# Cross-covariance attention and channel mix on one core: squares in quads, an earlier v, and units dealt out anew

## The chip, the cores and the metric

The kernel runs on one core of a Trainium2 chip. The metric is the device time of one execution in microseconds; the number given for a kernel is the median of several executions.

## The reference

The inputs are q, k and v of shape (4, 6208, 256) in float32, and the weights of a channel mix. For each of the four batches, with norms taken along the sequence of 6,208 rows:

```
qn, kn = q / (norm(q, axis=1) + 1e-6), k / (norm(k, axis=1) + 1e-6)
a = softmax(kn.T @ qn / tau)             # 256 x 256
x = v @ a
x_prev = x shifted by one row, zeros first
xk = mu_k * x + (1 - mu_k) * x_prev      # the same with mu_r for xr
out = sigmoid(xr @ w_r) * (relu(xk @ w_k) ** 2 @ w_v)
```

Here w_k is 256 x 1024, w_v 1024 x 256 and w_r 256 x 256. The output is float32. On the chip the matmuls run on bf16.

## The kernel before, in words

A batch has 12 blocks of 512 rows and 64 rows left over. The 48 blocks, and one block of the 4 x 64 leftover rows, go through the channel mix. Everything is issued in an order written out by hand.

**The head.** Batch 0's q and k are loaded through SP's queue in float32, cast by VectorE and ScalarE, and multiplied into the 256 x 256 covariance; its norms are made by TensorE from squares. A softmax follows, and the first x.

**The loop.** Pass i of the main loop has eight steps, j = 0 to 7. In it block i+1 is multiplied up: in each step `up` makes one 128 x 512 slice of the hidden layer (two matmuls into a `kT_ps` bank, of which there are three), and ScalarE's relu (L423) writes it to a tile `kr`. A step later, in every second step, `square` lets VectorE square the two slices of a `kr` tile into `kk` (L429). Block i is multiplied down: `down` makes, in two steps, w_r's product (L444) and w_v's over the eight slices of `kk` (L448) for 128 rows, in one of two `vr_ps` banks; `finish` takes a tanh on ScalarE (L457), a product on VectorE (L458), and the store through SP's queue. The squares of a block's last slices are made in step 0 of the pass that multiplies it down. For block i+2, `x_half` makes x (two halves in steps 0 and 2, L348 and L350), and VectorE makes the shifted difference `delta` (L394) and the two mixes `xk` and `xr` (L404).

**v.** `v_load` loads a block through POOL's queue with a cast to bf16, five passes before that block's pass, into one of five buffers. `v_transpose` turns it by a DMA transpose on SP's queue, four passes before, into one of four `vT` buffers. Blocks 0, 1 and 2 are turned by TensorE instead (`v_transpose_pe`, L327), through a `kT_ps` bank and a copy (L331).

**The next batches.** While the loop runs, batches 1 to 3 get their covariances. A batch is 49 units: 48 of 128 rows and one of the 64 leftover rows. `group_load` loads q and k of four units through POOL's queue with a cast, into a tile whose rows alternate q and k. `unit_matmul` makes two matmuls of 256 columns for a unit (L167), accumulating in one bank, `s_ps`. `unit_square` squares two units at once on ScalarE (L150) into float32, and `next_add` adds this to the running sum `acc` on VectorE (L154), in steps 1, 6 and 7 at most while no softmax is due. In which steps a pass issues a unit stands in `slots`; five units are multiplied ahead of pass 0. After a batch's last unit, `softmax_pieces` gives a list of pieces of which each step issues one: `evac` copies the covariance out, `fold` folds the sum of squares, `norms` to `spread` make and spread the inverse norms, then scaling, exponential, and `weigh`, which writes the matrix `a_sb` (L273) that `x_half` of the next batch reads.

The order of pieces and the slots, as they stand:

```
return [evac, None, fold, None, norms, roots, roots2, None, invert, None, spread, scale,
        None if bounded else top, exp, None, weigh]
...
elif i < 8:
    slots = (1, 2, 3, 4, 5, 7)
else:
    slots = (3, 5, 7) if (i - 8) % NB == 0 else (1, 3, 4, 5, 7) if (i - 8) % NB < 3 else (1, 3, 5, 7)
```

Of the kernel before, what the change touches and what calls it, by code (L numbers as in the profile page):

```python
# [18 lines left out]
def kernel(  # L19
# [76 lines left out]
    def order(b):  # L96
        g = list(range(len(sizes(b))))
        return [1, 2, 0] + g[3:] if b == 0 else g

# [10 lines left out]
    def group_load(b, g):  # L110
        rows, n = rows_of(b, g)
        qk = pq.tile([P, S, 2, C], BF16, name="qk", tag="qk", bufs=5)
        groups[b, g] = (qk,)
        if b == 0:
            qk2 = pq.tile([P, S, 2, C], BF16, name="qk2", tag="qk2", bufs=4)
            groups[b, g] += (qk2,)
            t_f = []
            for i, t in enumerate((q, k)):
                f = pq.tile([P, S, C], F32, name=f"f{i}", tag=f"f{i}", bufs=6)
                nc.sync.dma_start(f[:rows, :n], qk_src(t, b, g))  # L120
                t_f.append(f)
            groups[b, g] += tuple(t_f)
        else:
            for i, t in enumerate((q, k)):
                nc.gpsimd.dma_start(qk[:rows, :n, i, :], qk_src(t, b, g))  # L125

    def group_cast(b, g):
        rows, n = rows_of(b, g)
        qk, qk2, *t_f = groups[b, g]
        for i in range(2):  # L130
            nc.vector.tensor_copy(qk[:rows, :n, i, :], t_f[i][:rows, :n])  # L131
        for i in range(2):
            nc.scalar.activation(qk2[:rows, :n, i, :], t_f[i][:rows, :n], AF.Square)  # L133

    def unit_square(b, g, s):

        rows, n = rows_of(b, g)
        if s % 2:
            return
        qk = groups[b, g][0]  # L140
        if n == 1:
            t = pq.tile([P, 1, 2 * C], BF16, name="sq", tag="sq1", bufs=2)
            sums[b, "left"] = t
        elif (g, s) == (1, 0):
            t = pn.tile([P, 2, 2 * C], F32, name="acc", tag="acc", bufs=2)
            sums[b] = t
        else:
            t = pq.tile([P, 2, 2 * C], F32, name="sq2", tag=f"f{s // 2}", bufs=6)
            adds.append((now[0] + 2, b, t))
        nc.scalar.activation(t[:rows], qk[:rows, s:s + min(n, 2)].rearrange("p s i c -> p s (i c)"), AF.Square)  # L150

# [4 lines left out]
    def unit_matmul(b, g, s):  # L156
# [9 lines left out]
        for ih in range(2):  # L166
            nc.tensor.matmul(s_ps[:, ih, :], qk[:rows, s, 1, ih * P:(ih + 1) * P],  # L167
                             qk[:rows, s, 0, :], start=t0 and ih == 0, stop=te,
                             skip_group_check=True)
# [28 lines left out]
    def softmax_pieces(b):  # L198
# [20 lines left out]
        def fold():  # L219
            t = pq.tile([P, 2 * C], BF16, name="sq", tag="sq", bufs=1)  # L220
            nc.vector.tensor_tensor(t, sums[b][:, 0], sums[b][:, 1], op=OP.add)
            sums[b] = t

        def norms():
            bank[b] = ps.tile([P, 2 * C], F32, name="bank", tag="xT_ps", bufs=2)
            for t, rows in ((sums.pop((b, "left"))[:, 0], L), (sums.pop(b), P)):
# [64 lines left out]
        if b == 0:  # L291
            return [copies, gather, roots, evac, invert, spread, halves]

        return [evac, None, fold, None, norms, roots, roots2, None, invert, None, spread, scale,
                None if bounded else top, exp, None, weigh]

# [23 lines left out]

    def v_transpose_pe(i, evac):
# [7 lines left out]
        def go():  # L329
            vT = p2.tile([P, S, 2, P], BF16, name="vT", tag="vT", bufs=4)  # L330
            evac(vT, vT_ps)  # L331
# [80 lines left out]
    def up(i, fh):  # L412
# [5 lines left out]
        for dh in range(2):  # L418
            nc.tensor.matmul(kT_ps[:, :m], w_k_sb[:, dh, fh * P:(fh + 1) * P], xk[:, dh, :m],  # L419
                             start=dh == 0, stop=dh == 1)  # L420
        if fh % 2 == 0:
            st[i, "kr", fh // 2] = p2.tile([P, 2, M], BF16, name="kr", tag="kr", bufs=3)
        nc.scalar.activation(st[i, "kr", fh // 2][:, fh % 2, :m], kT_ps[:, :m], AF.Relu, scale=0.5 ** 0.5)  # L423

    def square(i, fh):
        m = size(i)
        if fh % 2:
            kr = st.pop((i, "kr", fh // 2))[:, :, :m]
            nc.vector.tensor_tensor(st[i, "kk"][:, fh - 1:fh + 1, :m], kr, kr, op=OP.mult)  # L429

# [90 lines left out]

    units = [(b, g, s) for b in range(1, B) for g in range(NB + 1) for s in range(sizes(b)[g])]
    loads = [(b, g) for b in range(1, B) for g in range(NB + 1)]
    AHEAD = 3
# [7 lines left out]
    def loads_upto():  # L532
# [3 lines left out]
        b, g, _ = units[min(n, len(units) - 1)]  # L536
        at = (b - 1) * (NB + 1) + g
        while loads and pos["ld"] <= at + AHEAD:
# [3 lines left out]
    chain = []  # L542
    FOLD = 14
    holds = [0]

    def unit(ahead=2):
# [9 lines left out]
        if u[1:] == (NB, S - 1):  # L556
            chain.extend(softmax_pieces(u[0]))
            holds[0] = u[0]

# [27 lines left out]

    early = units[:S + 1]
    pos["mm"] = pos["sq"] = S + 1

# [109 lines left out]
```

## Time and profile before

| | |
|---|---|
| median of 4 runs | 514.84 us (514.65 to 515.66) |
| the profiled execution's own time | 514.48 us |
| its span | 512.7 us |
| TensorE busy | 489.2 us, 95% of the span |
| VectorE busy | 457.2 us, 89% |
| ScalarE busy | 431.3 us, 84% |
| GpSimd busy | 104.5 us, 20% |
| granted TensorE clock | 1.00 |
| DMA packets, data moved | 143,734, 83.72 MB |

The profiled execution is one run; the span reaches from its first to its last instruction. Busy time is the time in which at least one instruction of an engine is under way. Matmuls are pipelined and overlap, and so do the ends of instructions on VectorE and ScalarE with the start of the next, so that the mean duration of an instruction is longer than its spacing to the next one. The first matmul of the main loop (pass -1) starts 44.8 us into the span.

### The profile page before, as it was taken

The numbers are of one execution on the slowest core, as the hardware profiler recorded it, in microseconds if no ns is written. First come the engines' busy times: TensorE is split into PE (matmuls) and PEld (weight loads), VectorE is DVE, ScalarE is ACT, GpSimd is POOL, SyncE is SP. The second block draws the span as 40 slices with busy tenths as digits, with TensorE's granted clock in tenths as the row PEclk, the third lists the DMA queues.
The fourth block names the chain that finished last, engine by engine and source line by source line (L and its number), as shares of the span: only waits on it lengthen the run. The fifth ranks groups of instructions, "written<-read, shape, count | busy, mean of one in ns | idle before, by whom it ended". The sixth has DMA issues, their size and how long they took to land.

```text
span 512.7 us, 9442 instructions
## 1 busy us (share of the span) xinstructions
PE 489.2 (95%) x3447; PEld 332.4 (65%) x3509; DVE 457.2 (89%) x788; ACT 431.3 (84%) x858; POOL 104.5 (20%) x143
## 2 busy tenths in 40 slices
PE   3989999999999999999999999999999999999996
PEld 1454566666666676677676667667666666666675
DVE  4557899999999999999999999999989787888884
ACT  5886999989888888888988889889877888878784
POOL 0046252322252222212152321210030110000000
PEclk9999999999999999999999999999999999999999
DMA  8999999999979999989899999964279756424123
GB/s 315 420 310 193 190 194 195 222 158 182 189 106 203 188 152 197 141 145 173 134 145 183 201 155 197 167 120 110 63 117 172 134 117 128 103 77 109 42 83 102
DMA packets 143734, 83.72 MB, mean 163 GB/s; under 512 B 51716, under 2 KB 140104, under 8 KB 143688
## 3 DMA queue, kind: packets, MB, share of 16 engines
q0 software_dynamic: 65808, 33.01, 51.9%
q1 hardware_dynamic: 77712, 49.98, 39.6%
q8 instruction: 27, 0.44, 0.4%
q10 hardware_dynamic: 168, 0.13, 0.1%
q14 instruction: 19, 0.16, 0.1%
HBM read 78.71 MB, written 25.43 MB: 203 GB/s over the span
## 4 chain that ended last, share of the span: by engine, by line
PE 68%; DVE 20%; DMA 5%; ACT 3%; issue 2%; SPq 1%; DVEq 0%; ACTq 0%
PE vr_ps L448 26%; PE kT_ps L419 23%; PE vr_ps L444 8%; PE xT_ps L348 6%; DVE acc L154 6%; DMA f<-in_k_dram 5%; DVE kk L429 5%; PE s_ps L167 4%; DVE xk L404 3%; DVE res L458 2%; DVE xr L404 2%; DVE delta L394 1%; ACT kr L423 1%; SPq L120 1%; ACT sq L150 1%
## 5 line engine op out<-in xcount | busy, mean ns | idle before, releaser
L423 ACT ACTIVATE kr<-kT_ps 128x512 bf16<-128x512 f32 (+1 forms) x392 | 233.9, 601 | 39.4 <-PE kT_ps L419 35.6
L448 PE MATMUL vr_ps<-w_v_sb,kk 128*128 128x256 bf16 x1536 | 231.8, 273 | 0.9 <-DVE kk L429 0.3
L419 PE MATMUL kT_ps<-xk,w_k_sb 128*128 128x512 bf16 (+1 forms) x725 | 218.4, 377 | 0.3 <-DVE xk L404 0.2
L448 PEld LDWEIGHTS <-kk 128*128 128x128 bf16 x1536 | 149.5, 98 | 60.3 <-DVE kk L429 3.2
L429 DVE TENSOR_TENSOR kk<-kr 128x1024 bf16<-128x1024 bf16 (+1 forms) x196 | 132.8, 677 | 3.7 <-ACT kr L423 2.8
L458 DVE SCALAR_TENSOR_TENSOR res<-res,vr_ps 128x256 f32<-128x256 f32 x192 | 79.4, 414 | 27.3 <-ACT res L457 26.9
L419 PEld LDWEIGHTS <-w_k_sb 128*128 128x128 bf16 x784 | 76.1, 98 | 28.7 <-issue 0.5
L154 DVE TENSOR_TENSOR acc<-acc,sq 128x1024 f32<-128x1024 f32 x69 | 83.9, 1216 | 0.0
L167 PE MATMUL s_ps<-qk 128*128 128x256 bf16 (+1 forms) x392 | 72.4, 285 | 4.9 <-DVE qk L131 4.8
L457 ACT ACTIVATE res<-vr_ps 128x256 f32<-128x256 f32 x192 | 75.5, 393 | 1.3 <-PE vr_ps L448 1.3
L444 PE MATMUL vr_ps<-w_r_sb,xr 128*128 128x256 bf16 x384 | 73.2, 272 | 3.3 <-DVE res L458 0.5
L350 ACT CAST xT<-xT_ps 128x512 bf16<-128x512 f32 x94 | 55.9, 594 | 23.2 <-PE xT_ps L348 23.0
L150 ACT ACTIVATE sq<-qk 128x1024 f32<-128x1024 bf16 (+1 forms) x72 | 75.2, 1046 | 0.0
L404 DVE SCALAR_TENSOR_TENSOR xr<-delta,mu_t,xT 128x512 bf16<-128x512 bf16 x96 | 71.3, 743 | 0.0
L404 DVE SCALAR_TENSOR_TENSOR xk<-delta,mu_t,xT 128x512 bf16<-128x512 bf16 x96 | 71.2, 743 | 0.0
L444 PEld LDWEIGHTS <-xr 128*128 128x128 bf16 x384 | 37.5, 98 | 45.6 <-issue 1.6
L125 POOL DMA_DIRECT2D qk<-in_q_dram x39 | 28.7, 735 | 181.4 <-ACT kr L423 140.6
L348 PE MATMUL xT_ps<-vT,a_sb 128*128 128x512 bf16 x188 | 56.1, 379 | 3.4 <-DVE a_sb L273 2.2
L311 POOL DMA_DIRECT2D v_bf<-in_v_dram x48 | 37.2, 776 | 63.9 <-DMA vT<-v_bf 61.6
L167 PEld LDWEIGHTS <-qk 128*128 128x128 bf16 (+1 forms) x392 | 38.3, 101 | 16.8 <-DVE qk L131 7.7
L394 DVE TENSOR_TENSOR delta<-xT 128x1024 bf16<-128x1024 bf16 x48 | 32.8, 684 | 0.1
L133 ACT ACTIVATE qk<-f 128x1024 bf16<-128x1024 f32 (+2 forms) x28 | 25.9, 948 | 7.1 <-DMA f<-in_q_dram 5.4
(82 smaller groups left out, 164.0 us busy)
## 6 DMA issues: line engine op xcount, KB each, us to landing
out_dram<-res SPq DMA_DIRECT2D x47, 512.0 KB, 4.2
v_bf<-in_v_dram POOLq DMA_DIRECT2D x48, 256.0 KB, 7.6
qk<-in_q_dram POOLq DMA_DIRECT2D x36, 256.0 KB, 6.0
qk<-in_k_dram POOLq DMA_DIRECT2D x36, 256.0 KB, 7.0
f<-in_q_dram SPq DMA_DIRECT2D x11, 512.0 KB, 8.4
f<-in_k_dram SPq DMA_DIRECT2D x11, 512.0 KB, 9.3
vT<-v_bf SPq DMA_TRANSPOSE x45, 7.3
f<-in_q_dram SPq DMA_DIRECT2D x2, 256.0 KB, 8.4
```

What stands on the lines that cost most here:

```text
L150: nc.scalar.activation(t[:rows], qk[:rows, s:s + min(n, 2)].rearrange("p s i c -> p s (i c)"), AF.Square)
L154: nc.vector.tensor_tensor(sums[b], sums[b], t, op=OP.add)
L167: nc.tensor.matmul(s_ps[:, ih, :], qk[:rows, s, 1, ih * P:(ih + 1) * P], qk[:rows, s, 0, :], start=t0 and ih == 0, stop=te, skip_group_che ...
L348: nc.tensor.matmul(xT_ps, a_sb[:, b, ih, dh * P:(dh + 1) * P], vT[:, :, ih, :], start=ih == 0, stop=ih == 1)
L404: nc.vector.scalar_tensor_tensor(o[:, dh], st[i, "d"][:, dh], mu[:, dh:dh + 1], st[i, "x"][:, dh, :M], op0=OP.mult, op1=OP.add)
L419: nc.tensor.matmul(kT_ps[:, :m], w_k_sb[:, dh, fh * P:(fh + 1) * P], xk[:, dh, :m], start=dh == 0, stop=dh == 1)
L423: nc.scalar.activation(st[i, "kr", fh // 2][:, fh % 2, :m], kT_ps[:, :m], AF.Relu, scale=0.5 ** 0.5)
L429: nc.vector.tensor_tensor(st[i, "kk"][:, fh - 1:fh + 1, :m], kr, kr, op=OP.mult)
L444: nc.tensor.matmul(vr_ps[:, D:], xr[:, dh, s * P:(s + 1) * P], w_r_sb[:, dh, :], start=dh == 0, stop=dh == 1)
L448: nc.tensor.matmul(vr_ps[:, :D], kk[:, fh, s * P:(s + 1) * P], w_v_sb[:, fh, :], start=fh == 0, stop=fh == 7)
L457: nc.scalar.activation(res[:, s], vr_ps[:, D:], AF.Tanh, scale=0.5)
L458: nc.vector.scalar_tensor_tensor(res[:, s], res[:, s], 1.0, vr_ps[:, :D], op0=OP.add, op1=OP.mult)
```

## The change

The change has five parts.

- The squares of relu: `kr` holds four slices instead of two, in two buffers instead of three, and VectorE squares four at once. For blocks 1 to 33 slice 0 is squared by ScalarE, right after its relu, and VectorE's first square takes slices 1 to 3. The block of leftover rows keeps pairs.
- q and k lie apart in their tile: all q rows of a partition, then all k rows. The tiles of squares follow this layout.
- v is loaded six passes ahead into six buffers and transposed five ahead into five. Block 3 is turned by TensorE, in pass 0. The loads ahead of the loop are issued in another order.
- The leftover rows come third in each batch, not first, and the units are dealt to other steps: four ahead of the loop, then 3, 6, 6, 7, 7, 7, 7 and so on.
- The softmax's list has 17 pieces in another spacing, with `fold` right after `evac`, and no unit is issued in the four steps after a batch's last.

```diff
-        return [1, 2, 0] + g[3:] if b == 0 else g
+        return [1, 2, 0] + g[3:]
...
-        qk = pq.tile([P, S, 2, C], BF16, name="qk", tag="qk", bufs=5)
+        qk = pq.tile([P, 2, S, C], BF16, name="qk", tag="qk", bufs=5)
...
-                nc.gpsimd.dma_start(qk[:rows, :n, i, :], qk_src(t, b, g))
+                nc.gpsimd.dma_start(qk[:rows, i, :n, :], qk_src(t, b, g))
...
-        return [evac, None, fold, None, norms, roots, roots2, None, invert, None, spread, scale,
-                None if bounded else top, exp, None, weigh]
+        return [evac, fold, None, None, norms, roots, roots2, None, None, invert, None, None, spread,
+                scale, *([] if bounded else [top]), exp, None, weigh]
...
-        v_bf = p2.tile([P, S, C], BF16, name="v_bf", tag="v_bf", bufs=5)
+        v_bf = p2.tile([P, S, C], BF16, name="v_bf", tag="v_bf", bufs=6)
...
-        vT = p2.tile([P, S, 2, P], BF16, name="vT", tag="vT", bufs=4)
+        vT = p2.tile([P, S, 2, P], BF16, name="vT", tag="vT", bufs=5)
...
-        if fh % 2 == 0:
-            st[i, "kr", fh // 2] = p2.tile([P, 2, M], BF16, name="kr", tag="kr", bufs=3)
-        nc.scalar.activation(st[i, "kr", fh // 2][:, fh % 2, :m], kT_ps[:, :m], AF.Relu, scale=0.5 ** 0.5)
+        if fh % 4 == 0:
+            st[i, "kr", fh // 4] = p2.tile([P, 4, M], BF16, name="kr", tag="kr", bufs=2)
+        kr = st[i, "kr", fh // 4][:, fh % 4, :m]
+        nc.scalar.activation(kr, kT_ps[:, :m], AF.Relu, scale=0.5 ** 0.5)
+        if fh == 0 and by_act(i):
+            nc.scalar.activation(st[i, "kk"][:, 0, :m], kr, AF.Square)
+
+    def by_act(i):
+        return 1 <= i < 3 * NB - 2
 
     def square(i, fh):
         m = size(i)
-        if fh % 2:
-            kr = st.pop((i, "kr", fh // 2))[:, :, :m]
-            nc.vector.tensor_tensor(st[i, "kk"][:, fh - 1:fh + 1, :m], kr, kr, op=OP.mult)
+        n = 4 if i < NBLK - 1 else 2
+        if fh % n == n - 1:
+            lo = 1 if fh == 3 and by_act(i) else fh % 4 + 1 - n
+            kr = st[i, "kr", fh // 4][:, lo:fh % 4 + 1, :m]
+            nc.vector.tensor_tensor(st[i, "kk"][:, fh // 4 * 4 + lo:fh + 1, :m], kr, kr, op=OP.mult)
...
-    FOLD = 14
-    holds = [0]
+    FOLD = 16 if bounded else 17
+    holds = [0, 0]
...
-            holds[0] = u[0]
+            holds[:] = u[0], now[0] + 4
...
-    next_load()
     v_load(1)
     next_load()
...
+    v_load(2)
     nc.gpsimd.dma_start(w_v_sb, moe_w_v.rearrange("(fo fi) d -> fi fo d", fi=P))
-    v_load(2)
-    next_load()
+    v_load(3)
...
-    early = units[:S + 1]
-    pos["mm"] = pos["sq"] = S + 1
+    early = units[:S]
+    pos["mm"] = pos["sq"] = S
...
-            if j == 0 and 3 <= i + 5 < NBLK - 1:
-                v_load(i + 5)
+            if j == 0 and i + 6 < NBLK - 1:
+                if i < 0:
+                    next_load()
+                v_load(i + 6)
...
-            if j == 5 and 3 <= i + 4 < NBLK - 1:
-                v_transpose(i + 4)
+            if i == 0 and j == 6:
+                v_transpose_pe(3, nc.vector.tensor_copy)()
+            if j == 5 and 4 <= i + 5 < NBLK - 1:
+                v_transpose(i + 5)
...
-            if (i, j) in ((0, 1), (0, 5), (1, 3)):
-                unit_square(*early[{(0, 1): 0, (0, 5): 1, (1, 3): 3}[i, j]])
+            if (i, j) in ((0, 1), (0, 3)):
+                unit_square(*early[{(0, 1): 0, (0, 3): 2}[i, j]])
...
-                slots = (3, 5, 7)
-            elif i == 1:
-                slots = (1, 2, 4, 5, 7)
-            elif i < 8:
-                slots = (1, 2, 3, 4, 5, 7)
+                slots = (5, 6, 7)
+            elif i < 7:
+                slots = (1, 2, 3, 4, 5, 7) if i < 3 else (1, 2, 3, 4, 5, 6, 7)
+            elif i == 7:
+                slots = (1, 2, 7)
+            elif (i - 7) % NB == 0:
+                slots = (5, 7)
             else:
-                slots = (3, 5, 7) if (i - 8) % NB == 0 else (1, 3, 4, 5, 7) if (i - 8) % NB < 3 else (1, 3, 5, 7)
-            if j in slots and pos["mm"] < len(units):
+                slots = (1, 3, 4, 5, 7) if (i - 7) % NB in (1, 3, 6, 9) else (1, 3, 5, 7)
+            if j in slots and pos["mm"] < len(units) and now[0] >= holds[1]:
                 unit()
```

More of the change, by code (lines that the diff above doesn't have):

```diff
@@ L130, in group_cast @@
         for i in range(2):
-            nc.vector.tensor_copy(qk[:rows, :n, i, :], t_f[i][:rows, :n])
+            nc.vector.tensor_copy(qk[:rows, i, :n, :], t_f[i][:rows, :n])
         for i in range(2):
@@ L141, in unit_square @@
         if n == 1:
-            t = pq.tile([P, 1, 2 * C], BF16, name="sq", tag="sq1", bufs=2)
+            t = pq.tile([P, 2, 1, C], BF16, name="sq", tag="sq1", bufs=2)
             sums[b, "left"] = t
         elif (g, s) == (1, 0):
-            t = pn.tile([P, 2, 2 * C], F32, name="acc", tag="acc", bufs=2)
+            t = pn.tile([P, 2, 2, C], F32, name="acc", tag="acc", bufs=2)
             sums[b] = t
         else:
-            t = pq.tile([P, 2, 2 * C], F32, name="sq2", tag=f"f{s // 2}", bufs=6)
+            t = pq.tile([P, 2, 2, C], F32, name="sq2", tag=f"f{s // 2}", bufs=6)
             adds.append((now[0] + 2, b, t))
-        nc.scalar.activation(t[:rows], qk[:rows, s:s + min(n, 2)].rearrange("p s i c -> p s (i c)"), AF.Square)
+        nc.scalar.activation(t[:rows], qk[:rows, :, s:s + min(n, 2)], AF.Square)
     def next_add():
@@ L166, in unit_matmul @@
         for ih in range(2):
-            nc.tensor.matmul(s_ps[:, ih, :], qk[:rows, s, 1, ih * P:(ih + 1) * P],
-                             qk[:rows, s, 0, :], start=t0 and ih == 0, stop=te,
+            nc.tensor.matmul(s_ps[:, ih, :], qk[:rows, 1, s, ih * P:(ih + 1) * P],
+                             qk[:rows, 0, s, :], start=t0 and ih == 0, stop=te,
                              skip_group_check=True)
@@ L219, in fold @@
         def fold():
-            t = pq.tile([P, 2 * C], BF16, name="sq", tag="sq", bufs=1)
-            nc.vector.tensor_tensor(t, sums[b][:, 0], sums[b][:, 1], op=OP.add)
+            t = pq.tile([P, 2, C], BF16, name="sq", tag="sq", bufs=1)
+            nc.vector.tensor_tensor(t, sums[b][:, :, 0], sums[b][:, :, 1], op=OP.add)
             sums[b] = t
@@ L225, in norms @@
             bank[b] = ps.tile([P, 2 * C], F32, name="bank", tag="xT_ps", bufs=2)
-            for t, rows in ((sums.pop((b, "left"))[:, 0], L), (sums.pop(b), P)):
+            for t, rows in ((sums.pop((b, "left")).rearrange("p i s c -> p (i s c)"), L),
+                            (sums.pop(b).rearrange("p i c -> p (i c)"), P)):
                 for i in range(4):
@@ L329, in go @@
         def go():
-            vT = p2.tile([P, S, 2, P], BF16, name="vT", tag="vT", bufs=4)
+            vT = p2.tile([P, S, 2, P], BF16, name="vT", tag="vT", bufs=5)
             evac(vT, vT_ps)
@@ L520 @@
             v_load(0)
-    units = [(b, g, s) for b in range(1, B) for g in range(NB + 1) for s in range(sizes(b)[g])]
-    loads = [(b, g) for b in range(1, B) for g in range(NB + 1)]
+    units = [(b, g, s) for b in range(1, B) for g in order(b) for s in range(sizes(b)[g])]
+    loads = [(b, g) for b in range(1, B) for g in order(b)]
     AHEAD = 3
@@ L536, in loads_upto @@
         b, g, _ = units[min(n, len(units) - 1)]
-        at = (b - 1) * (NB + 1) + g
+        at = (b - 1) * (NB + 1) + order(b).index(g)
         while loads and pos["ld"] <= at + AHEAD:
```

## The prediction

> **What bounds the kernel now.** I read the page first (TensorE busy 489.2 of 512.7 us, VectorE 457.2), then cut the span at the starts of the loop's passes and asked for the busy time of each engine in these stretches, then the chain and the waits inside them. Pass i multiplies block i+1 up and block i down. Four passes, columns as in the page's engines (busy us and instruction count), then clock, DMA share, GB/s:
>
> ```profile
> 81.60:92.00 10.40, 10.27 (x74) 6.95 (x73) 10.40 (x17) 9.32 (x19) 1.47 (x2) 1.00 1.38 195
> ...
> 154.20:165.20 11.00, 10.04 (x72) 6.85 (x72) 10.96 (x21) 9.64 (x19) 2.23 (x3) 1.00 1.37 211
> ...
> 184.50:194.00 9.50, 9.45 (x69) 6.61 (x68) 9.29 (x16) 8.39 (x18) 2.82 (x4) 1.00 1.00 152
> ...
> 404.80:413.50 8.70, 8.65 (x61) 5.89 (x61) 7.27 (x14) 7.08 (x16) 0.78 (x1) 1.00 0.64 122
> ```
>
> TensorE looks full in all four, so its busy share tells nothing; the length of a pass does. The last has no covariance unit, the third 4, the first 6. One pass is 20 matmuls of 512 columns and 40 of 256. In the chain a pair of the former takes 0.43 us and five of the latter 0.55, so a pass needs 20 x 0.216 + 40 x 0.109 = 8.68 us, and each unit (two of 256) 0.218 more. Without units the pass is 8.7 us long and with four 9.56 (floor 9.55): TensorE at its floor. With six the floor is 9.99, yet passes 2 to 6 take 10.39. Why, the chain says:
>
> ```profile
> 82.14 1.14 DVE acc L154
> ...
> 86.01 0.33 DVE res L458
> 86.34 1.14 DVE acc L154
> 87.48 0.60 DVE kk L429
> 88.08 0.66 DVE xr L404
> 88.74 0.33 DVE res L458
> 89.07 0.60 DVE delta L394
> ...
> 91.27 0.67 DVE xk L404
> ```
>
> Pure VectorE. These times are spacings to the next instruction (the profile's means run about 0.08 longer, since the ends overlap). A pass is one delta 0.60, four squares 2.41, two xk and two xr 2.65, four res 1.32 = 6.98 us, and 1.135 for each running add; with three adds 10.39, the length of the pass. So VectorE bounds passes 1 to 8 (61 to 144 us) and pass 10 (11.0 us: three adds and the last softmax piece, 6.98 + 3.41 + 0.53). At the end of each softmax TensorE also waits for it:
>
> ```profile
> PEld L348 <- DVE a_sb L273: 3.5, 6, 1.2
> PE xT_ps L348 <- DVE a_sb L273: 2.2, 3, 0.9
> PE xT_ps L348 <- DMA vT<-v_bf: 0.4, 1, 0.4
> ```
>
> The third is block 3's transpose, landing late, once. Summing length less floor, passes 0 to 34 hold about 9 us to win; the passes after are at the floor and the 44.8 us head is a stream of loads.
>
> [...] the trace has the shape:
>
> ```profile
> L150 ACT ACTIVATE sq<-qk 64x512 bf16<-64x512 bf16 x3 | 1.9, 618 | 0.0
> ```
>
> [...]
>
> **The change, part by part.**
> *Squares in quads.* Blocks 1 to 33: four DVE squares (2.41 us) become one of 1,536 elements and one of 2,048. No such size is in the trace; at 0.52 ns per element and a fixed 0.07 (from 0.60 for 1,024) I take 0.87 + 1.135 = 2.00, so 0.40 less per pass; the other blocks save 0.14. Bounds: nothing saved (if a long one runs slower), or 0.45. Added on ScalarE: one Square of 512, 0.52, plus about 0.11 because it reads what the instruction ahead has just written (in the head an xk that follows its delta so started 0.72 after it, not 0.60): 0.63, bounds 0.5 to 0.9. Behind it on ScalarE stand the xT copy, the next relu and the tanh; VectorE and TensorE wait for these. ScalarE holds 8 relus 3.95, two xT 0.96, four tanh 1.10, a copy 0.08 and 0.47 per unit: 8.0 us with four units before, 8.6 of 9.56 after; with seven 10.04 of 10.21. It fits, narrowly there. The later squares of a block come in one piece at the next pass's first step: 1.13 instead of 0.60, but the pair before is gone from the queue ahead of it. At 186.60 that pair's square started 1.3 us ahead of its reader; the quad would begin about 0.6 earlier and end with some 0.5 to spare. Cost nothing while VectorE has slack; without it, up to 0.5 a pass.
>
> *Units regrouped.* 4 instead of 5 before the loop, then 3, 6, 6, 7, 7, 7, 7, 2: batch 1 ends in pass 7 step 2, not step 7; batch 2 at the end of pass 18, not 19; batch 3 in pass 30, not 31. No unit is added or lost. The running adds are still three a pass at most, so VectorE needs 6.58 + 3.41 = 9.99 in passes 1 to 6, against floors of 9.99 (6 units) and 10.21 (7): both engines level, TensorE ahead. The softmax chain grows from 16 to 17 pieces but starts 5, 8 and 10 steps earlier, so its last piece comes some 5 or more steps ahead of its use, not one: the a_sb waits go. What is late next there is VectorE in pass 7 (three adds and the fold, about 11.0 us of work in a pass with floor 9.4), which I let leak 0.5.
> The four-step hold on new units spares a wait on the single s_ps bank; it costs no work.
>
> *Block 3 on TensorE.* Eight transposes of 128 columns, 8 x 0.056 = 0.45, and a VectorE copy 0.60 in pass 0. VectorE is busy 7.7 of 9.9 there, which hides the copy; if not, TensorE waits 0.8 as it did for block 2's. Off: a DMA transpose, its SP issue and the 0.4 wait. Pass 0 is ScalarE's: squares 4 x 0.95 + 0.52, relus, copies, and now the new Square: 10.5 us of work against 9.9 long before. I put it at 10.2.
>
> *v one block further ahead, six and five buffers.* The same POOL and SP issues, earlier: POOL's 0.78 per v load and two of 0.73 per group move past each other in the head. w_v comes behind one v block (256 KB, some 1.3 us by the gaps between landings): it landed at 48.3, would at about 49.6, and is first read at 53.7. Group 1 moves ahead of the leftover rows and needs nothing later. Cost nothing; if that cover went, 1 us once. TensorE waits nowhere else on v, so nothing is won either.
> *q and k apart.* Each row of a partition becomes one 2 KB piece instead of four of 512 B: 36,864 packets of 143,734 fall to about 9,200. No engine waits on these loads after the head: nothing, either way.
>
> **The sum**, by pass. Pass -1: 6.0 (6.2). Pass 0: 10.2 (9.9). 1 and 2: 10.1 each. 3 to 6: 10.3 each. 7: 9.9; 8: 10.3; 9: 9.7; 10: 9.85; 11: 9.6. Together 126.9, before 130.1 (44.8 to 174.9): 3.2 off. Passes 12 to 23: 12 x 8.68 + 50 x 0.218 + 0.7 for the softmax's and leftover matmuls + 0.3 of stalls = 116.1, before 117.2: 1.1 off. Passes 24 to 34: 11 x 8.68 + 29 x 0.218 + 1.0 = 102.8, before 104.0: 1.2 off. The last pass waits for one quad more, +0.2 (estimate); ScalarE's fuller queue, +0.5 over 33 passes (estimate). Net 4.8. The profiled execution took 514.48 around a span of 512.7, 0.36 under the median of the runs; so its like would be 509.7 and the median 514.84 - 4.8 = **510.1 us**.
>
> **The rivals.**
> *A, as summed* (0.68): 510.1, own range 508 to 512.
> *B, ScalarE hands part of it back* (0.14): with 8.6 to 10.0 us in each pass it lags after the 0.95 us squares, and TensorE meets it at the next free kT_ps bank, 0.08 a pass: 33 x 0.08 = 2.7, so 512.8. For: passes 3 to 6 have 0.2 us to spare. Against: with 8.9 of 10.4 us of work in the six-unit passes of before, no wait of TensorE for ScalarE is listed after the head.
> *C, slower* (0.11): the new Square at the first step of a pass holds up the xT copy and tanh queued behind it; the res release of vr_ps and the down products follow, every time. Before, ScalarE idled 0.58 and 0.29 around this place (185.2 and 186.2 us), which should swallow 0.63. If it does not, 0.3 a pass is 9.9 us: 520. It decides from 4.8 / 33 = 0.15 a pass.
> *D, the quads save nothing* (0.07): long DVE squares cost in proportion. Then passes 1 to 6 stay at 10.4 and only the earlier softmax counts: about 512.4. [...]
>
> **Numbers.** About 0.2% (1 us) is what a measurement of this kernel can tell from no change. Faster by more: nearly all of A, 0.09 of B, 0.06 of D = 0.82; within: 0.07; slower: C, 0.11. The range 506.8 to 514.2 takes in A with both ends of the unknown costs (all 9 us won less 1; ScalarE's 0.9) and B and D; it leaves out C and a little at each end.
>
> **What would show it.** Squares of 128x2048 spaced 1.13 and of 128x1536 0.87; passes 3 to 6 near 10.3 us with seven units, with VectorE no longer without a gap; no PE wait on a_sb L273's successor; pass 10 and 22 under 9.9; packets near 116,000. I am wrong if ScalarE is without gaps in passes 1 to 33 and TensorE waits for kT_ps or vr_ps, if quads are the wait of the down products, or if passes with four units exceed 9.6.

## The result, and the profile after

The changed kernel takes **516.96 us** (median of 44 runs, 513.95 to 529.54) where the kernel before took 515.70 beside it (63 runs): a ratio of **1.0027, 95% interval 1.0014 to 1.0040**. By this ratio it is slower by 1.4 us; 4.8 us less had been forecast. Ratios here leave out executions that took over 1.5% more than the kernel's shortest (five of these 44), medians do not. The profiled execution took 516.47 us, its span 514.7.

Busy times in the stretches that answer to those shown of before; columns as there. The first line is pass 7 of before, which the prediction did not show; the others are passes 3, 7, 13 and 18 of after:

```profile
123.20:133.50 10.30, 10.19 (x73) 6.93 (x73) 10.30 (x17) 9.21 (x19) 1.47 (x2) 1.00 1.14 191
```

```profile
82.30:92.50 10.20, 10.15 (x76) 7.14 (x75) 10.20 (x15) 9.84 (x20) 2.21 (x4) 1.00 1.24 194
123.30:135.70 12.40, 9.84 (x74) 6.59 (x74) 12.37 (x18) 10.21 (x22) 0.24 (x1) 1.00 1.30 158
185.30:195.10 9.80, 9.69 (x71) 6.77 (x72) 9.08 (x14) 9.05 (x19) 1.86 (x3) 1.00 1.23 141
233.50:244.80 11.30, 9.79 (x73) 6.78 (x73) 9.62 (x14) 9.19 (x20) 1.06 (x2) 1.00 1.22 168
```

Pass 3 has seven units in 10.2 us where it had six in 10.4, and pass 13 five in 9.8 where it had four in 9.6. Those are gains, as forecast. But pass 7 takes 12.4 us with three units where it took 10.3 with six, and in it VectorE is busy 12.37 us and TensorE 9.84; and pass 18 takes 11.3, with no engine full. The lengths of the passes, from the start of one's first up matmul to the next one's, are the measure of what follows. Each kernel has one profile; where two kernels issue the same work their passes agree within some 0.02 us, but for the places told below. (The stretch ahead of the loop differs from profile to profile, 44.1 to 47.4 us.)

| passes | forecast | before | after |
|---|---|---|---|
| 1 | 10.1 | 10.32 | 10.71 |
| 2 to 6 | 51.3 | 52.03 | 51.03 |
| 7 | 9.9 | 10.31 | **12.41** |
| 9 | 9.7 | 10.40 | 10.40 |
| 10 and 22 | | 21.82 | 19.56 |
| 18 | | 9.68 | **11.29** |
| 21 | | 10.21 | 10.95 |
| whole loop, -1 to 47 | 463.1 | 467.93 | 469.29 |

Against the forecast the loop is 6.2 us too long. Pass 7 is 2.5 of it, pass 18 some 1.5, pass 21 some 1.2 (as pass 9, about 9.7 had been meant), pass 9 0.7 and pass 1 0.6; the others give 0.3 back.

**Pass 7.** From the chain of waits in the pass (start, us, what):

```profile
124.16 0.46 DVE acc L154
...
127.42 1.14 DVE acc L154
...
129.14 1.22 DVE acc L154
130.35 0.33 DVE res L467
130.69 0.60 DVE delta L395
131.29 1.15 DVE acc L154
...
132.46 0.69 DVE sq L221
133.15 0.87 DVE kk L438
134.01 0.66 DVE xk L405
134.68 0.34 DVE res L467
...
135.06 0.38 PE vr_ps L453 x2
```

Batch 1 now ends in step 2 of this pass, so the running adds that are left are forced in ahead of `fold` (`sq` L221), and `fold` stands ahead of the squares and of the `res` that frees a `vr_ps` bank. There are four adds here, not the three of the prediction: both kernels make 69, after makes one in pass 0 and three in each of passes 1 to 6, and four are left of batch 1. With four, the prediction's own prices give VectorE 6.58 + 4 x 1.135 + 0.61 for the fold = 11.7 us of work in a pass that it put at 9.4 for TensorE. VectorE works through it in this order and TensorE waits for the last. Its waits in the pass (engine, line, what it waited for: us in total, times, longest) say so:

```profile
PE vr_ps L453 <- DVE res L467: 1.9, 2, 1.4
...
PE bank L229 <- DVE sq L221: 0.6, 1, 0.6
```

**Pass 18.** Here TensorE waits for a transpose of v, which the chain follows back 23.7 us. First the wait, then the chain:

```profile
PE xT_ps L349 <- DMA vT<-v_bf: 1.5, 1, 1.5
```

```profile
212.51 23.69 DMA vT<-v_bf
...
236.24 0.59 PE xT_ps L349 x2
```

**The transfers.** In the DMA view between 175 and 300 us, with the median time from issue to landing last, first the kernel before, then after:

```profile
vT<-v_bf SPq DMA_TRANSPOSE x13, 7.3
```

```profile
out_dram<-res SPq DMA_DIRECT2D x12, 512.0 KB, 14.9
...
vT<-v_bf SPq DMA_TRANSPOSE x13, 18.0
```

The stores took 6.8 before. The same bytes are moved, in fewer and larger packets: 38,160 in POOL's queue, 65,808 before, so the page of after has

```profile
DMA packets 115029, 83.45 MB, mean 162 GB/s; under 512 B 50660, under 2 KB 102184, under 8 KB 114984
```

### The profile page after: what moved, and what is told of

It is laid out like the page before. It is cut to its first block, busy times and chain, and to the rows that moved or that the text cites. A ratio compares the mean times of both kernels' runs of the same rounds, so it can differ in the third digit from the quotient of the medians.

```text
span 514.7 us, 9328 instructions
## 1 busy us (share of the span) xinstructions
PE 489.2 (95%) x3455; PEld 333.2 (65%) x3517; DVE 442.2 (86%) x693; ACT 447.0 (87%) x891; POOL 88.7 (17%) x143
## 3 DMA queue, kind: packets, MB, share of 16 engines
q0 software_dynamic: 38160, 33.01, 47.8%
## 4 chain that ended last, share of the span: by engine, by line
PE 72%; DVE 10%; DMA 10%; ACT 5%; issue 2%; SPq 0%; DVEq 0%; ACTq 0%
PE vr_ps L457 27%; PE kT_ps L420 24%; PE vr_ps L453 8%; PE xT_ps L349 6%; PE s_ps L167 5%; DMA f<-in_k_dram 5%; DMA vT<-v_bf 5%; DVE kk L438 2%; DVE xk L405 2%; DVE acc L154 2%; ACT kr L425 2%; DVE res L467 1%; DVE delta L395 1%; ACT res L466 1%; ACT sq L150 1%
## 5 line engine op out<-in xcount | busy, mean ns | idle before, releaser
L467 DVE SCALAR_TENSOR_TENSOR res<-res,vr_ps 128x256 f32<-128x256 f32 x192 | 79.6, 415 | 45.4 <-ACT res L466 44.6
L438 DVE TENSOR_TENSOR kk<-kr 128x1536 bf16<-128x1536 bf16 (+2 forms) x100 | 109.7, 1097 | 0.3 <-ACT kr L425 0.2
L167 PE MATMUL s_ps<-qk 128*128 128x256 bf16 x392 | 73.1, 287 | 4.1 <-DVE qk L131 4.1
L150 ACT ACTIVATE sq<-qk 128x1024 f32<-128x1024 bf16 x72 | 75.8, 1055 | 0.0
L125 POOL DMA_DIRECT2D qk<-in_q_dram x39 | 21.0, 537 | 168.8 <-ACT kr L425 90.5
L167 PEld LDWEIGHTS <-qk 128*128 128x128 bf16 x392 | 38.6, 102 | 16.2 <-DVE qk L131 7.4
## 6 DMA issues: line engine op xcount, KB each, us to landing
out_dram<-res SPq DMA_DIRECT2D x47, 512.0 KB, 6.6
f<-in_q_dram SPq DMA_DIRECT2D x11, 512.0 KB, 8.4
f<-in_k_dram SPq DMA_DIRECT2D x11, 512.0 KB, 9.4
```

The costliest lines, as they stand in the source:

```text
L150: nc.scalar.activation(t[:rows], qk[:rows, :, s:s + min(n, 2)], AF.Square)
L167: nc.tensor.matmul(s_ps[:, ih, :], qk[:rows, 1, s, ih * P:(ih + 1) * P], qk[:rows, 0, s, :], start=t0 and ih == 0, stop=te, skip_group_che ...
L438: nc.vector.tensor_tensor(st[i, "kk"][:, fh // 4 * 4 + lo:fh + 1, :m], kr, kr, op=OP.mult)
L467: nc.vector.scalar_tensor_tensor(res[:, s], res[:, s], 1.0, vr_ps[:, :D], op0=OP.add, op1=OP.mult)
```

## The experiments

Two theories share the loss. The **order theory** (D in the expectations, for DVE, which is VectorE, and S for softmax pieces in step 0; the prediction's D is another): pieces of the softmax and adds stand in VectorE's queue ahead of what TensorE waits for. The **packet theory** (P): the 2 KB packets of q and k hold up the transposes and stores in SP's queue. The rivals: ScalarE's added Square, the quads themselves, and the reading of the new layout by TensorE and ScalarE. The names that begin with e and r keep v's transposes; those with p put plain copies between the same tiles in their place, so that no late transpose hides VectorE's order. In the p kernels v is therefore not turned. The diffs are excerpts: other uses of the same tile, and the counter `FOLD` where a list changes, follow.

### The packets

**e1_interleaved**: after, with q and k alternating in the tile as before.

```diff
-        qk = pq.tile([P, 2, S, C], BF16, name="qk", tag="qk", bufs=5)
+        qk = pq.tile([P, S, 2, C], BF16, name="qk", tag="qk", bufs=5)
...
-                nc.gpsimd.dma_start(qk[:rows, i, :n, :], qk_src(t, b, g))
+                nc.gpsimd.dma_start(qk[:rows, :n, i, :], qk_src(t, b, g))
```

> The changed kernel with q and k interleaved in their tile again (loads land in 512 B packets), all else kept. Theory P (2 KB packets of the q/k loads hold up the DMA transposes of v behind them): transposes land in a median of 7 to 11 us as before, not 15; pass 18 falls from 11.3 to about 9.6 us; the spread of the runs shrinks to that of before; 1.5 to 3 us faster than the changed kernel, so about 513. Theory V (the slower landings come from v being asked for one block further ahead, more transfers being under way at once): transposes stay near 15 us and the time near 517. Pass 7 (12.4 us) is untouched under both.

**e3_padded**: after, q and k apart, but each row padded by 16 elements, so that the pieces are 512 B again but all q rows still come ahead of all k rows.

```diff
-        qk = pq.tile([P, 2, S, C], BF16, name="qk", tag="qk", bufs=5)
+        qk = pq.tile([P, 2, S, C + 16], BF16, name="qk", tag="qk", bufs=5)
...
-                nc.gpsimd.dma_start(qk[:rows, i, :n, :], qk_src(t, b, g))
+                nc.gpsimd.dma_start(qk[:rows, i, :n, :C], qk_src(t, b, g))
```

> The changed kernel with q and k apart, but each row of 256 padded to 272 elements, so that the loads land again in 512 B packets while every engine reads the same split layout. If the packet size is the cause: landings and time as in the interleaved run (about 513). If it is the reading of the split layout by ScalarE and TensorE: time stays near 517.

e1 measured 516.38 against 516.85 for before, ratio 0.9989 (0.9978 to 1.0000); e3 516.58, 0.9988 (0.9977 to 0.9999). Both are some 0.38% under after's 1.0027: about 2.0 us, within the 1.5 to 3 expected (the time of about 513 was not reached). Pass 18 is 9.78 in both, not 11.29; pass 7 stays at 12.41. In e3's DMA view from 175 to 300 us:

```profile
vT<-v_bf SPq DMA_TRANSPOSE x13, 10.3
```

Since e3 keeps the layout and gives up only the large packets, it is their size that costs in after, not the reading. The executions show it too. The shortest of after, e1 and e3 agree (513.95, 514.22, 514.18), but of the 39 of after that its ratio counts 11 lie above 518.2, and none of the 22 of e1 or of the 22 of e3. What the packets cost thus differs from one execution to the next.

**e2_before_apart**: the kernel before with only q and k apart (the edit of e1 the other way round, in before).

> The kernel before with q and k apart in the tile and nothing else (2 KB packets, v four passes ahead as before). Theory P: transposes land in a median of about 15 us, some over 20, where only some 13 us of lead (1.4 passes from issue to use) are there: TensorE waits several times for vT, 5 to 25 us slower than before. Theory V: nothing changes, within 1 us of before.

523.91, ratio 1.0129 (1.0108 to 1.0149). All of it is in pass 1, 19.07 us instead of 10.32. First its wait, then the stretch that follows it (the clock is the figure before the last two):

```profile
PE xT_ps L349 <- DMA vT<-v_bf: 6.4, 1, 6.4
```

```profile
68.00:75.00 7.00, 5.20 (x18) 2.75 (x19) 2.82 (x4) 2.05 (x4) 1.53 (x3) 0.52 0.56 125
```

The three transposes issued between 50 and 80 us landed after 13.3 us in the median; TensorE waited 6.4 us for block 3's, and from late in that wait, 68.3 us, its clock was half for 6.8 us. Several such waits and a median landing of about 15 us had been expected. Neither came. Between 175 and 300 us:

```profile
vT<-v_bf SPq DMA_TRANSPOSE x13, 6.7
```

So the large packets alone do not slow the transposes there: with the order of before they land after 6.7 us against 7.3, with that of after after 18.0 against 10.3. Which part of the new order the packets need for their harm, no run separates. Turning block 3 on TensorE, which I had costed at nothing and credited with 0.4 us, takes this one wait out of after; what after would lose without it was not run.

**r4_v_ahead**: the kernel before with v one block further ahead, six and five buffers, block 3 on TensorE.

```diff
-            if j == 0 and 3 <= i + 5 < NBLK - 1:
-                v_load(i + 5)
+            if j == 0 and 4 <= i + 6 < NBLK - 1:
+                v_load(i + 6)
...
-            if j == 5 and 3 <= i + 4 < NBLK - 1:
-                v_transpose(i + 4)
+            if i == 0 and j == 6:
+                v_transpose_pe(3, nc.vector.tensor_copy)()
+            if j == 5 and 4 <= i + 5 < NBLK - 1:
+                v_transpose(i + 5)
```

> The kernel before with v loaded and transposed one block further ahead, six and five buffers, and block 3 turned by TensorE in pass 0; nothing else. The prediction put this at no cost: 0.998 to 1.002, passes as before within 0.1 us. If the earlier loads of v are what lifts the landing of the transposes from 7.3 to the 10.1 seen with the old packets, the median between 175 and 300 us is 9 to 11 us here; if it is the regrouping of the loads of q and k, it stays near 7.3.

516.57 against 516.73, ratio 0.9997 (0.9988 to 1.0006): nothing, as forecast. The transposes land after 7.7 us in the median, so the earlier v alone does not slow them either. In the profile pass -1 grew by 1.15 us (TensorE waited 1.9 for two loads of v in the head) and pass 0 shrank by 0.5.

### VectorE's order

**e4_adds**: after, with a running add allowed in step 4 too and no forced adds ahead of `fold`.

```diff
-            if adds and adds[0][0] <= now[0] and (j in (1, 6, 7) or adds[0][1] == holds[0] and chain):
+            if adds and adds[0][0] <= now[0] and j in (1, 4, 6, 7):
```

> The changed kernel with the running adds allowed in steps 1, 4, 6 and 7 of every pass, and no longer in every step while a softmax is due. Theory D (pass 7 is long because a backlog of adds, three in a row of steps, and the fold run on VectorE ahead of res and the squares): pass 7 falls from 12.4 to 10 to 10.5 us, passes 3 to 6 grow by up to 0.3 each since VectorE then needs 10.5 there; net 0.5 to 2 us faster. Rival (pass 7 is long for another reason, such as the norms waiting for the fold): pass 7 stays over 11.5.

527.3, ratio 1.0193 (1.0162 to 1.0223). The profile is of one of its two shorter executions (523.06; the other four took 526.9 to 528.1). Pass 7 fell to 9.76, as the order theory said. But passes with an add in step 4 grew, those with four units to 10.29 and passes 1 to 6 together from 61.7 to 65.4, since that add, behind the step's square, holds up a `res`:

```profile
PE vr_ps L453 <- DVE res L467: 8.1, 13, 1.3
```

The same mechanism, in another place, at 0.6 us a time.

**p1_before, p2_after**: before and after, with the copies.

```diff
-        nc.sync.dma_start_transpose(vT.rearrange("c s h p -> c (s h) p"), v_bf.rearrange("p s c -> p (s c)"))
+        nc.sync.dma_start(vT.rearrange("c s h p -> c (s h p)"), v_bf.rearrange("p s c -> p (s c)"))
```

> The kernel before with every DMA transpose of v replaced by a plain copy between the same tiles (the turning of v is left out, so x is made from v unturned; all else is issued as before). It takes the late transposes out of the comparison. Both theories: passes 1 to 34 as in the kernel before (10.4 us with six units, 10.9 in passes 10 and 22), within 1 us of before.

> The changed kernel with the same plain copies in place of the transposes. Theory P: pass 18 falls from 11.3 to 9.7 us and the spread of the runs goes; theory D and S: pass 7 stays at 12.4, 9 at 10.4 to 10.5, 21 at 10.9. Against the plain-copy kernel before: about the ratio of the interleaved run, 0.999. If it came out 1% faster than that kernel, DMA would be the whole story.

p1: 516.0, ratio 0.9980 (0.9969 to 0.9992); p2: 515.21, 0.9973 (0.9957 to 0.9988). With no transposes the late one of pass 18 is gone (9.78), but passes 7, 9 and 21 stay at 12.41, 10.40 and 10.95. The loop is 467.76 and 467.53: all other parts of the change together gain 0.2 us of the forecast 4.8.

**p3_before_quads**: before with copies and only the quads and ScalarE's Square. **p4_after_pairs**: after with copies and the pairs of before. The edits are the hunk on `kr` and `square` in the diff above, put in and taken out.

> The plain-copy kernel before with the squares in quads and one of eight on ScalarE, nothing else. Theory Q (the quads do what the sum said: VectorE needs 9.99, not 10.39, in a six-unit pass): passes 2 to 7 take about 10.0 us, passes 10 and 22 lose some 0.4: 2 to 3.5 us faster than the plain-copy kernel before. Rival (long squares in two lumps hold up res and the down products and eat what they save): passes 2 to 7 stay over 10.3, within 1 us.

> The plain-copy changed kernel with squares in pairs on VectorE and none on ScalarE. Theory Q: VectorE bounds passes 1 to 8 again at 10.4 to 10.6 us, pass 7 stays over 11.5: 2 to 5 us slower than the plain-copy changed kernel. Rival (the lumps of the quads are what fails in passes 7, 9 and 21): those passes fall to under 10.5, and the time is at or under that kernel's.

p3: 514.81, ratio 0.9955 (0.9936 to 0.9974). Passes 3 to 7 are 9.99 to 10.1 instead of 10.39: the 0.40 us per VectorE-bound pass, in full. It loses elsewhere: passes 1 and 2 have a quad that comes too late (10.73 and 10.50), and pass -1 (7.84) waits for v in the head. (Pass 33 grew by 0.5, but pass 34 gave it back.) p4: 516.1, 0.9982 (0.9970 to 0.9993). Its loop is only some 0.9 us longer than p2's; pass 7 is 13.09, passes 3 to 6 10.4. In after, where the order costs more, the quads are worth less.

**p8_no_act**: p2 with all squares on VectorE (`by_act` always False).

> The plain-copy changed kernel (v not turned) with no square on ScalarE: all quads of 2,048 on VectorE (+0.27 us there per pass, -0.63 on ScalarE). If ScalarE's fuller queue costs the kernel something (rival B), it is faster in passes with four units or in 1 and 2. If ScalarE is free, as summed: the same in passes of four and five units, and longer by 0.2 to 0.3 us in passes 1 and 2, and 7 longer.

517.69, ratio 1.0042 (1.0025 to 1.0059), the loop 1.9 us longer than p2's, in the passes that VectorE bounds (3 to 6 by 0.6 together, 7 by 0.5, 9 by 0.46). Passes with four units grew by at most 0.1. But pass 1 fell from 10.71 to 10.41. In after's pass 1 a tanh, a `res`, an add and the quad follow one another (62.08, 62.58, 62.91 and 64.05 us), and TensorE waits 0.33 us for the quad; without the Square, ScalarE comes out of pass 0 earlier. So ScalarE's Square gains 1.9 us, with the 0.3 that it costs in pass 1 taken off.

**p5_step0**: p2, with a softmax piece among `fold`, `invert`, `scale` and `weigh` put off by a step when it falls into step 0, where the quad stands.

```diff
-                if len(chain) == FOLD and any(e[1] == holds[0] for e in adds):
+                if (j == 0 and getattr(piece, '__name__', '') in ('fold', 'invert', 'scale', 'weigh')
+                        or len(chain) == FOLD and any(e[1] == holds[0] for e in adds)):
```

> The plain-copy changed kernel (v not turned), and a softmax piece for VectorE (fold, invert, scale, weigh) that falls on step 0 of a pass is put off by one step, so that it stands behind the quad of the block to be multiplied down, not ahead of it. Theory S (in passes 9, 21 and 32 the piece ahead of the quad is what TensorE waits for): pass 9 from 10.4 to about 9.7, pass 21 from 10.95 to about 9.7, pass 31 or 32 by 0.3, so about 2 us faster than the plain-copy changed kernel. Rival (VectorE is simply full there): the sum of passes 8 to 11 and 20 to 23 stays within 0.5 us.

515.96, ratio 1.0002 (0.9986 to 1.0018) against 0.9973 of p2. This is the place in pass 21 of after, by the timeline (start, us, engine, line, operation, count, in brackets the idle time before it):

```profile
266.98 0.16 DVE L272 RECIPROCAL sm<-sm 128x2 f32<-128x2 f32 x1
...
267.17 0.61 DVE L274 TENSOR_SCALAR a_sb<-s_sb,sm 128x256 bf16<-128x256 f32 x2
...
267.70 1.21 DVE L438 TENSOR_TENSOR kk<-kr 128x2048 bf16<-128x2048 bf16 x1
...
268.97 0.61 PE L457 MATMUL vr_ps<-w_v_sb,kk 128*128 128x256 bf16 x4 [1.00 <-DVE kk L438]
```

`weigh` takes the 0.7 us ahead of the quad, and TensorE idles 1.0 us for the quad. Putting it off brought pass 21 from 10.95 to 10.23; but pass 22 grew by 0.5, and pass 9 from 10.40 to 11.42: there the exponential on ScalarE waited 0.9 us for the scaling that was put off, and the tanh that a `res` reads stood behind it. The loss moved, in pass 9 to another engine's queue.

**p6_six**: p2, with six units in each of passes 1 to 7 and the softmax list of before.

```diff
-        return [evac, fold, None, None, norms, roots, roots2, None, None, invert, None, None, spread,
-                scale, *([] if bounded else [top]), exp, None, weigh]
+        return [evac, None, fold, None, norms, roots, roots2, None, invert, None, spread, scale,
+                None if bounded else top, exp, None, weigh]
...
-                slots = (1, 2, 3, 4, 5, 7) if i < 3 else (1, 2, 3, 4, 5, 6, 7)
+                slots = (1, 2, 3, 4, 5, 7)
...
-                slots = (1, 2, 7)
+                slots = (1, 2, 3, 4, 5, 7)
```

> The plain-copy changed kernel (v not turned) with six units in each of passes 1 to 7, so that batch 1 ends in the last step of pass 7, and the softmax's list of before (16 pieces). Theory D (the seven-unit passes leave VectorE a backlog of adds that pass 7 pays for): pass 7 falls from 12.4 to about 10.0, passes 3 to 6 to 10.0 each, pass 8 stays near 10.3: passes 3 to 9 about 3 us shorter together. Rival (the fold and norms cost TensorE 2 us wherever they fall): the 2 us turn up in pass 8.

511.9, ratio 0.9923 (0.9904 to 0.9942). Pass 7 is 9.99 and passes 3 to 6 are 40.09 together. But passes 10 and 22 are 10.76: `weigh` is again one step ahead of its reader, and TensorE waits as before the change:

```profile
PE xT_ps L349 <- DVE a_sb L274: 0.6, 1, 0.6
```

**p7_phased**: p6, with one None more ahead of `invert`, and those ahead of `spread` and of `exp` dropped.

> As the six-unit run (plain copies, v not turned), and the softmax's list spaced so that, with all three batches ending in a pass's last step, no piece for VectorE falls on step 0 (fold in step 2, invert 1, scale 3, weigh 6). Theories D and S together: passes 7, 9, 10, 19 to 23 and 31 to 34 within 0.5 us of the floor, the loop about 5 us shorter than in the plain-copy changed kernel, which is what the prediction's sum gave. Rival (VectorE is full): no shorter than the six-unit run.

516.67, ratio 1.0018 (1.0002 to 1.0034). My design failed: passes 9, 21 and 33 are 11.7 to 11.9, because `spread`, a TensorE piece, now comes one step after the VectorE piece that it reads:

```profile
PE bank L252 <- DVE rq_d L247: 1.6, 1, 1.6
```

**p9_six_early**: p6, only without the None ahead of `exp`, so that `weigh` comes a step earlier.

> As the six-unit run (plain copies, v not turned; list of before), but with the pause between scaling and exponential dropped, so that the last piece, weigh, stands in step 6 of passes 9, 21 and 33 and not in step 7; the distance of two steps from invert to spread is kept. Theory S (a piece for VectorE just ahead of the quad of step 0 holds up the down products): passes 10 and 22 fall from 10.76 to 10.1 and pass 33 from 9.7 to about 9.1, pass 9 and 21 stay at 10.0: the loop about 2 us shorter, 463 us, which is what the prediction's sum came to (463.1). Rival (VectorE is full around a softmax): passes 9 and 10 together stay at 20.7 us.

511.18, ratio 0.9890 (0.9866 to 0.9914). Passes 10 and 22 are 10.09, the wait on `a_sb` is gone, the loop is 463.97. Pass 33, expected to fall too, stayed at 9.68.

### Both together

**r1_six_padded, r2_six_apart, r3_six_interleaved**: p9 with v's transposes, and rows padded as in e3, apart as in after, and alternating as in e1.

> The changed kernel with its DMA transposes, with rows of q and k padded to 272 elements (so its q and k loads fall into 512 B packets as before), six units in each of passes 1 to 7, and the softmax list of the kernel before less the None ahead of exp. If VectorE's order and the 2 KB packets are the two places where the forecast gain went, both are mended here: the kernel with plain copies in the place of the transposes ran at 0.989 of the kernel before, the transposes being worth about 0.2% in the kernel before, so 0.988 to 0.994 (about 511 us), loop 463.9 to 465, passes 3 to 7 near 10.0, passes 10 and 22 near 10.1. If late transposes come back with the earlier loads of v whatever the packets, a wait of TensorE on vT of 1 us or more shows and the ratio is 0.995 or above.

> The same with rows not padded, so 2 KB packets for q and k. If packets cost what the two layouts differed by in the changed kernel, 0.3 to 0.4% above the padded one, and median landing of the transposes between 175 and 300 us about 18 us, with a wait of TensorE on vT in or near pass 18. If the packets cost only because the order of the changed kernel put its loads badly: within 0.1% of the padded one.

> The same with q and k interleaved again in the tile, unpadded. Both theories of the packets give the time of the padded one within 0.15%; landing of transposes about 10 us. If the padding itself costs or saves reading time, it differs by more.

r3: **511.03 us** against 516.73, ratio **0.9890 (0.9871 to 0.9908)**. r1: 511.71, 0.9901 (0.9885 to 0.9916). The loops are 464.22 and 464.23, no wait on `vT` is left after the head, and pass 7 of r3 has neither VectorE's excess nor TensorE's gap:

```profile
122.20:132.20 10.00, 10.00 (x74) 7.06 (x73) 10.00 (x16) 9.69 (x21) 1.49 (x2) 1.00 1.37 194
```

r2 is the case with the large packets: its profiled execution has the same passes (loop 464.21), yet the three executions that its ratio counts took 511.0, 511.6 and 515.0 and three more 518.9 to 524.2, where the four of r1 and of r3 stay within 510.8 to 512.0. The ratio, 0.9917 (0.9885 to 0.9948), cannot tell it from the others. Its transposes land late, in the median after

```profile
vT<-v_bf SPq DMA_TRANSPOSE x14, 12.2
```

where r1 has 4.5 and r3 5.2. That looks like after against e1 and e3, where some executions are long and others are not, but six executions do not show it. In r2's profile no transpose was late enough to be waited for, so the expected wait near pass 18 is not there, and no profile shows where its long executions lost their time. The ratio of r3 is worth 5.7 us, the loops of the two profiles differ by 3.7: the profile of before is of an execution of 514.48, and where the others, 515.9 to 517.9 beside r3, are longer no profile shows. r3 is the version to keep: the quads, ScalarE's Square, block 3 on TensorE and the earlier v, with the old layout, six units a pass and the list of p9.

## Why the prediction was wrong

**The sum of a pass stood for its order.** This is the larger error, up to 4.4 us (p2's loop 467.5 against the forecast 463.1). I wrote that pass 7 has "three adds and the fold, about 11.0 us of work in a pass with floor 9.4" and "let leak 0.5". Two things fail here. It was four adds, so 11.7 us of work. And there was no ground for 0.5: VectorE's surplus can be put off only if nothing that TensorE needs stands behind it, and `res`, the triple and `fold` itself all do. The pass took 12.41 us, 3.0 over TensorE's floor instead of 0.5. e4 and p6, each with fewer adds left for this pass, bring it to 9.76 and 9.99. The same step failed for pass 21, where `weigh` stands ahead of the quad (0.7 us, by p5). For pass 9 it is read from the profile alone: `scale` stands ahead of the quad. Of pass 1's 0.6, p8 puts 0.3 down to ScalarE's Square. The sentence on the quad in step 0 gave the price, "without it, up to 0.5 a pass", but I took the slack from 186.60 us, a place with no softmax piece ahead of it. e4, p5 and p7 show how narrow this is: moving one piece by a step or two costs or gains 0.5 to 2 us a pass. r1 to r3, with other units per pass and another list, come within 1.1 us of the forecast loop: 464.2.

**"q and k apart … nothing, either way".** The argument, that no engine waits on these loads after the head, was nearly true (one weight load in pass 1 waits 0.4 us for q) and not enough: the transposes, which TensorE does wait for, landed after 10.3 us with these loads in 512 B packets (e3) and after 18.0 with 2 KB ones (after). e1 and e3 put this at 0.38%, 2.0 us. How the size acts is not shown: e2 has the 2 KB packets too, and there the transposes landed after 6.7 us.

**What was right.** The squares: spacings of 0.869 and 1.135 us for the triple and the quad (0.87 and 1.135 forecast) and 0.537 on ScalarE (0.52), with about 0.1 more of waiting for its relu (266.37 us to 266.98 in pass 21; a relu's spacing to the next is 0.49). The groups of after, with each instruction's mean, which runs some 0.08 above the spacing:

```profile
L438 DVE TENSOR_TENSOR kk<-kr 128x2048 bf16<-128x2048 bf16 x63 | 76.7, 1218 | 0.3 <-ACT kr L425 0.2
L438 DVE TENSOR_TENSOR kk<-kr 128x1536 bf16<-128x1536 bf16 x33 | 31.3, 950 | 0.0
...
L427 ACT ACTIVATE kk<-kr 128x512 bf16<-128x512 bf16 x33 | 20.8, 630 | 1.1
```

The profile of before has the same prices. On VectorE a bf16 delta of 256 elements and squares of 512 and 1,024 have means of 287, 418 and 683 ns: 0.52 ns for each further element, and 0.15 us that does not grow with them. On ScalarE the square of 64x512 at 54.22 us is followed by a relu at 54.74. On TensorE matmuls of 256 and 512 columns follow one another after 0.109 and 0.216 us, their means being 273 and 379 ns.

The 0.40 us per pass (p3), passes 2 to 6, the end of the waits on `a_sb`, block 3's copy being hidden, v ahead at nothing (r4), and the number of packets also came as forecast.

**The rivals.** B, ScalarE handing back 0.08 in each pass, is refuted by p8: it hands back 0.3 in pass 1 and nothing that shows later. C, the Square holding up xT and tanh, did not happen: four-unit passes are 9.56 with it (p2) and 9.56 to 9.64 without (p8). D, that quads save nothing, is refuted by p3, and the three means of before, with their fixed 0.15 us, had spoken against it. The forecast had no rival for the mechanism that decided, a piece in VectorE's queue ahead of a release; C had its form, on the wrong engine, and that the kernel came out slower, as C said, is no credit to C.

**Left open**: how large packets act, and where the long executions lose their time. The granted clock alone does not tell: executions of after of 515.4 and of 521.6 us both had 0.996 in the mean. Nor is it known why the stretch ahead of the loop varies. In after's profile 3.41 us of half clock fall into it (32.04 to 35.45 us) and its loop starts at 45.4 us; in that of before none do, and its loop starts at 44.8. Half of 3.41 us is 1.7, the spread of all profiles 3.3 (44.1 to 47.4), so this is part of it at most.

## What to carry to other kernels

A balance of work per pass says what is reachable, not what will happen. Here the loop of p2 took 467.5 us where 463.1 had been summed. For each operation that is merged, moved or forced, write down what stands behind it in its engine's queue and who waits for it, in the very step where it lands. And a change in the packets of one queue can change the latency of another, in one order of issue (18.0 us against 10.3) and not in the next (6.7 against 7.3): look at the median landing of transfers that nothing seemed to tie to it, and at the spread of the executions.

## What the hardware showed that I had not expected

The same gap cost more in one profile than in another. In e1's profile, after pass 7's waits of 0.5 and 1.4 us, TensorE's granted clock fell to half for 3.4 us (136.8 to 140.2), and pass 8 took 11.89 us; in e3, with the same waits, it did not, and pass 8 took 10.21, 1.7 us less. The same two microseconds of the pass in e1 and in e3:

```profile
136.70:138.70 2.00, 2.00 (x11) 1.13 (x9) 2.00 (x4) 0.60 (x1) 1.58 (x1) 0.53 0.00 0
```

```profile
135.00:137.00 2.00, 2.00 (x15) 1.21 (x14) 2.00 (x4) 1.19 (x3) 1.51 (x1) 1.00 0.01 1
```

TensorE looks equally full in both; only the clock and the number of matmuls tell, 0.53 and 11 against 1.00 and 15. p5 had it too (0.55 from 136 to 138 us, pass 8 11.89). In the profile of before the clock was never half between 18.2 and 512.7 us.

The 3.4 us come back elsewhere. In the head of after the half clock also lasted 3.413 us, and in e2 the 6.8 us are twice that. The stretches at full clock in the clock records are 494.933 us long in before, 17.067 and 477.866 in after, each within 0.05 us of a multiple of 3.413 (145, 5 and 140 times). What decides whether a gap is followed by half clock these runs do not show: e1 and e3 have the same waits of 0.5 and 1.4 us, and only e1 lost the 1.7 us.
